# Turning operands by DMA in other portions, and an image's reduction spread over other tiles, in a fused attention and gated feed-forward kernel

## Chip, core and metric

The kernel runs on one core of one Trainium2 chip. The metric is the device time of one execution in microseconds. Before the change three executions took 1033.67, 1035.01 and 1040.39 us; the median is 1035.01 us. The profiled execution took 1032.41 us, of which 1030.6 us lie between its first and its last instruction.

## What is computed

Four images of 384 x 32 pixels with 128 channels serve as keys and values; each is averaged over 4 x 4 pixels and multiplied by a 128 x 128 matrix, which leaves 768 tokens per image. Each image has 12288 queries. Attention is followed by a feed-forward layer with a rectified gate, 1536 wide.

```python
kv_pool = kv.reshape(B, H // r, r, W // r, r, C).mean(axis=(2, 4))
k = v = kv_pool.reshape(B, -1, C) @ w_sr
s = scale * (q @ k.transpose(0, 2, 1))
a = np.exp(s - s.max(-1, keepdims=True))
x = (a / a.sum(-1, keepdims=True)) @ v
gate = np.maximum(x @ w_gate, 0.0)
out = (gate * (x @ w_val)) @ w_out
```

## The kernel before

The 49152 queries are cut into 96 tiles of 512, 24 for each image, and the tiles into groups of four (GRP). A tile passes through a software pipeline. In the main loop (L717), step k works on several tiles at once: scores and exponentials of tile k, weighted values of tile k - 2 (`kV`), the two input projections and the gate of tile k - 3 (`kF`), and the output projection of tile k - 4 (`kO`). The order of all this within a step is a list of words written out by hand; STEADY (L92) serves nearly all steps, FIRST (L82) the first two, DRAIN and LAST the end. The first four tiles and the first image are done before the loop by another list, OPENING. Each word is issued in the order of the list, so that each engine's own queue has the order of the list too.

The words and lines that matter here are these.

- `s0` to `s3`: `score_block` multiplies 128 queries by the 768 keys (L357, two matmuls) into a two-bank PSUM tile. `e0` to `e3`: `exp_block` takes the exponential on ScalarE (L362), whose output `a` has queries on the partitions.
- `a_turn` (L389) turns `a` by a transposing DMA on the SyncE (SP) queue, so that tokens lie on the partitions, as the product with the values needs it. Before the change it follows each `e` word, for one block of 128 queries: 6 blocks of 128 x 128, four times in a step.
- `x0` to `x5`: `values` (L399) multiplies the turned exponentials by the values. In STEADY the first of these, `x1`, stands some four tenths into the step.
- `q_load` (L144) fetches the queries of a group on the GpSimd (POOL) queue, with a cast to 16 bits. `q_turn` (L154) turns a whole group, 16 blocks of 128 x 128, by one DMA on the SP queue, in the second step of the group before.
- `out_turn` and L736 store the output; of the four pieces of a step in the steady part, two go over the SP queue and two over POOL.
- `image_step` (L704) prepares the next image beside the tiles of the present one, in three pairs of 128-token chunks, a pair every four steps. It counts from `at`, which is the step within the image less 6, and for a pair `since = at - 4 * pair`. Loads (L223, two for each of `since` 0 and 1, 512 KB each) go over the SP queue. Sums over pixels (L233 to L241, one half at `since` 2 and one at 3) run on POOL. Word `tb` transposes 32 x 32 blocks on VectorE and stores them to DRAM (L321), and L712 brings them back in four pieces, on the SP queue. Words `P` and `pk` (L298, L307) project and keep the keys. At `since` 8 `turn_values_dma` (L332) turns two chunks of keys into values, by two transposing DMAs on the SP queue.

So the SP queue carries, in one order: the turns of exponentials, of queries and of values, the loads of the image, the trip of the pooled image through DRAM, and half of the output. It takes them strictly one after the other, and each waits there for what it reads. `a` and `aT` have four buffers each, `qT` three, `q16` (the queries before the turn) two, and `kv_in` (the loaded image lines of a pair) two. In the built program each DMA of the SP queue also waits for the landing of the one issued eight before it.

Of the kernel before, what the change touches and what calls it, by code (L numbers as in the profile page):

```python
# [10 lines left out]
FP16 = mybir.dt.float16  # L11
# [5 lines left out]
def kernel(  # L17
# [23 lines left out]
    nc = tc.nc  # L41

    B, N, C = q.shape
# [8 lines left out]
    NS = T // 128  # L52
    NST = N // T
    NT = B * NST
    GRP = 4
# [45 lines left out]
    work = ctx.enter_context(tc.tile_pool(name="work", bufs=2))  # L101
# [19 lines left out]
    q16s, qTs, q32s, q_banks = {}, {}, {}, {}  # L121
# [11 lines left out]
    def q_load(g):  # L133
        if not 0 <= g < NG:
            return
        b, n0 = divmod(g * GRP * T, N)
        q16 = work.tile([128, GRP * NS, C], FP16, tag="q16", bufs=2)
        rows = q[b, n0 : n0 + GRP * T, :]
        if g == NG - 1:
            nc.gpsimd.dma_start(q16, rows.rearrange("(p s) c -> p s c", p=128))  # L140
        else:
            rows = rows.rearrange("(i t j s) c -> j t i s c", i=GRP, t=32, s=NS)
            for j in range(4):
                nc.gpsimd.dma_start(  # L144
                    q16[32 * j : 32 * (j + 1)].rearrange("t (i s) c -> t i s c", i=GRP), rows[j]
                )
        q16s[g] = q16

    def q_turn(g):
        if not 0 <= g < NG:  # L150
            return
        q16 = q16s.pop(g)
        qT = work.tile([128, GRP * NS, 128], FP16, tag="qT", bufs=3)
        nc.sync.dma_start_transpose(qT, q16.rearrange("p s c -> p (s c)"))  # L154
        qTs[g] = qT

    def q_load_pair(i):
        q32 = work.tile([128, 2, NS, C], FP32, tag="kv_s2", bufs=2, name="q32")
# [44 lines left out]
    kv16 = const.tile([128, B, NJC, 2 * C + 16], FP16)  # L203
    kv_in = {}

    def kv_load(b, pair, lines=range(r), queues=(nc.sync,)):
        if (b, pair) not in kv_in:
            if (b, pair) == (0, NJC // 2 - 1):
                kv_in[b, pair] = [
                    work.tile([128, NS * J // 2], FP32, tag="a16", bufs=4, name="kv_line")[  # L210
                        :, 0 : 2 * r * C
                    ].rearrange("p (h dw c) -> p h dw c", h=2, dw=r)
                    for dh in range(r)
                ]
            else:
                lines_in = work.tile([128, r, 2, r, C], FP32, tag="kv_in", bufs=2, name="kv_in")
                kv_in[b, pair] = [lines_in[:, dh] for dh in range(r)]
        parts = kv_in[b, pair]
        rows = kv[b, pair * 2 * HC : (pair + 1) * 2 * HC].rearrange(
            "(hp dh) (wp h dw) c -> dh hp wp (h dw c)", dh=r, h=2, dw=r  # L220
        )
        for dh in lines:
            queues[dh % len(queues)].dma_start(  # L223
                parts[dh].rearrange("p h dw c -> p (h dw c)"), rows[dh]
            )
# [3 lines left out]
    def pool_pixels(eng, b, pair, h):  # L229
        parts = kv_in[b, pair]  # L230
        s2 = work.tile([128, 2, r, C], FP32, tag="kv_s2", bufs=2)
        for i in range(2):
            eng.tensor_tensor(s2[:, i], parts[2 * i][:, h], parts[2 * i + 1][:, h], op=ALU.add)  # L233
        s1 = work.tile([128, r, C], FP32, tag="kv_s1", bufs=2)
        eng.tensor_tensor(s1, s2[:, 0], s2[:, 1], op=ALU.add)
        c2 = work.tile([128, 2, C], FP32, tag="kv_c2", bufs=2)
        eng.tensor_tensor(c2, s1[:, 0:2], s1[:, 2:4], op=ALU.add)
        if h == 0:
            s3s[b, pair] = work.tile([128, 4, 2, 32], FP32, tag="kv_s3", bufs=2, name="kv_s3")
        c4 = c2.rearrange("p i (j c) -> p i j c", c=32)  # L240
        eng.tensor_tensor(s3s[b, pair][:, :, h], c4[:, 0], c4[:, 1], op=ALU.add)  # L241
# [54 lines left out]
    def project(b, pair):  # L296
        pr = project_banks[b, pair] = wide.tile([128, 1024], FP32, tag="wide", name="wide_ps")
        nc.tensor.matmul(  # L298
            pr[:, 0:256].rearrange("c (i h p) -> c i h p", i=4, h=2), w_sr_f32,
            kv_Ts.pop((b, pair)), start=True, stop=True,  # L300
        )
# [25 lines left out]
            for j in range(4)  # L327
        ]

    def turn_values_dma(b, pair):  # L330
        for jc in (2 * pair, 2 * pair + 1):
            nc.sync.dma_start_transpose(kv16[:, b, jc, C : 2 * C], kv16[:, b, jc, 0:C])  # L332


    aTs, x_banks, x16s, xTs, rinvs = {}, {}, {}, {}, {}
    hTs, o_banks, o_sbs, vals = {}, {}, {}, {}
# [50 lines left out]
    def a_turn(k, s0, s1):  # L387
        aT = aTs[k].rearrange("k j t -> k (j t)").rearrange("k (x p) -> k x p", p=128)
        nc.sync.dma_start_transpose(  # L389
            aT[:, s0 * NJC : s1 * NJC], a16s[k][:, s0:s1, :].rearrange("p s j -> p (s j)")  # L390
        )
# [93 lines left out]
    def out_proj(k, fb):  # L485
        if k >= NT - 3:
            if fb == 0:
                o_banks[k] = bank([128, NS, 128])
            for s in range(NS):
                out_add(k, fb, s, o_banks[k][:, s, :], fb == 0 and s == 0)  # L490
            return
        if fb == 0:
            o_banks[k] = bank([128, T])
        nc.tensor.matmul(  # L494
            o_banks[k], wo16[:, fb, :], hTs[k][:, fb, :], start=fb == 0, stop=fb == NFB - 1
        )
# [205 lines left out]
    out_moves, moves, spread = [], [], []  # L702

    def image_step(b, at, step):  # L704
        for pair in range(NJC // 2):
            since = at - 4 * pair
            if since in (0, 1) and step in (2, 8):
                kv_load(b, pair, [2 * since + step // 8])
            elif since in (2, 3) and step == 3:
                pool_pixels(nc.gpsimd, b, pair, since - 2)  # L710
            elif since == 5 and moves and step > 4:
                nc.sync.dma_start(*moves.pop())  # L712
            elif since == 8 and step == 1:
                turn_values_dma(b, pair)

    last = NT + LAG - 1
    for k in range(LEAD, last + 1):  # L717
        g, ph = divmod(k, GRP)
        if k == GRP:
            nc.sync.dma_start_transpose(  # L720
                qTs[1][:, 2 * NS :], q16s.pop(1)[:, 2 * NS :].rearrange("p s c -> p (s c)")
            )
        if ph == 1:
            q_turn(g + 1)
            q_load(g + 2)
        b = k // NST + 1
        at = k % NST - 6
        kO, kF, kV = k - LAG - 1, k - LAG, k - 2
        words = FIRST if kV < LEAD else STEADY if k < NT else DRAIN if k < last else LAST
        for word in words:  # L730
            head, n = word.rstrip("0123456789"), int(word.lstrip("abcdefghijklmnopqrstuvwxyzADPT") or 0)
            if head == "o":
                out_proj(kO, n)
                for queue in (nc.gpsimd, nc.sync):
                    if out_moves and n >= 2:
                        queue.dma_start(*out_moves.pop())  # L736
                if spread:
                    spread_scales(*spread.pop(0))
                if b < B:
                    image_step(b, at, n)  # L740
            elif head == "oT":
                if kO < NT - 3:
                    out_moves = out_turn(kO)
                elif k < last:
                    out_scale(kO, nc.vector, slice(0, NS))
                    out_store(kO, slice(0, NS))
            elif head in ("v", "y", "g", "h"):
                if kF < NT:
                    {"v": value_proj, "y": keep_value, "g": gate_proj, "h": gated}[head](kF, n)
            elif head in ("s", "e"):  # L750
                if k < NT:
                    {"s": score_block, "e": exp_block}[head](k, n)
                    if head == "e":
                        a_turn(k, n, n + 1)
            elif head == "r":
                if LEAD < k <= NT and k % 2 == 0:
                    invert(k - 2)
                    spread += [(k - 2, j) for j in range(4)]
            elif head in ("tb", "P", "pk"):
                pair, since = divmod(at - 5 if head == "tb" else at - 7, 4)  # L760
                if b < B and 0 <= pair < NJC // 2 and since == 0:
                    if head == "tb":
                        moves.extend(turn_blocks(b, pair))
                    elif head == "P":
                        project(b, pair)
                    else:
                        keep_projected(b, pair)
            elif LEAD <= kV < NT:
                if head == "x":
                    values(kV, n)  # L770
                else:
                    keep_values(kV)
# [33 lines left out]
```

The softmax here doesn't subtract the row's maximum and nothing guards it: scores larger than these inputs give would overflow.

## Time and profile before

| engine | busy us | share of the span |
|---|---|---|
| TensorE, matmuls (PE) | 1019.9 | 99% |
| ScalarE (ACT) | 920.8 | 89% |
| VectorE (DVE) | 862.9 | 84% |
| GpSimd (POOL) | 524.5 | 51% |
| TensorE, weight loads (PEld) | 489.2 | 47% |

| issued on the SP queue | count | what one moves | median us from issue to landing |
|---|---|---|---|
| turn of exponentials, L389 | 368 | 6 blocks of 128 x 128 | 3.4 |
| output, L736 | 216 | 64 KB in most | 2.3 |
| load of the image, L223, in the loop and before it | 42 | 512 KB | 4.7 |
| turn of queries, L154 | 22 | 16 blocks | 8.9 |
| turn of values, L332 | 18 | 1 block | 2.6 |

The TensorE clock was granted in full all the time. A busy share is an average over the whole span: it doesn't say whether an engine lost time in a few places, nor how full a queue is. The time in which the SP queue issues a DMA isn't counted as busy time of an engine; it shows only in the timeline, as the duration of the issuing instruction (named SPq).

### The profile page before, as it was taken

The page shows a single profiled execution, that of the slowest core. Times are in us where ns is not written, and L with a number is a line of the kernel's source. Part 1 is how long each engine was busy: PE and PEld are TensorE (multiplying, and loading weights), DVE is VectorE, ACT ScalarE, POOL GpSimd, SP SyncE. Part 2 cuts the span into 40 slices and gives each one's busy share as a digit, 9 for nine tenths or more (in the row PEclk, how much of TensorE's full clock was granted, in tenths as well). Part 3 has the DMA queues.
Part 4 walks back from the last instruction along what each step waited for, and adds up shares of the span by engine and source line. Part 5 has one row for each costly group of instructions (what it writes and reads, how often), then busy time and mean ns, then how long its engine had stood idle before and what let it go on. Part 6 is the DMA issues. An engine that isn't in the chain of part 4 may idle for free.

```text
span 1030.6 us, 18011 instructions
## 1 busy us (share of the span) xinstructions
PE 1019.9 (99%) x5048; PEld 489.2 (47%) x5048; DVE 862.9 (84%) x1432; ACT 920.8 (89%) x1931; POOL 524.5 (51%) x1308
## 2 busy tenths in 40 slices
PE   9999999999999999999999999999999999999998
PEld 6444444444444444444444444444444444444445
DVE  2888888888888888887888888888888888888888
ACT  5999998889999999998999999989899999999986
POOL 3586584834444657564433666566343543343332
PEclk9999999999999999999999999999999999999999
DMA  9998898997989989889888998998997786857541
GB/s 328 130 160 162 173 169 185 143 151 128 160 131 194 155 169 160 159 136 151 145 137 138 185 184 153 180 138 133 147 160 128 137 123 124 145 105 120 103 85 45
DMA packets 480500, 153.55 MB, mean 149 GB/s; under 512 B 456720, under 2 KB 470544, under 8 KB 480400
## 3 DMA queue, kind: packets, MB, share of 16 engines
q1 hardware_dynamic: 458368, 126.10, 67.7%
q0 software_dynamic: 21600, 25.19, 16.0%
q10 hardware_dynamic: 432, 1.11, 0.3%
q8 instruction: 40, 0.66, 0.3%
q14 instruction: 60, 0.49, 0.2%
HBM read 53.94 MB, written 26.35 MB: 78 GB/s over the span
## 4 chain that ended last, share of the span: by engine, by line
PE 96%; DMA 1%; DVE 1%; ACT 1%; issue 0%; SPq 0%; DVEq 0%
PE bank_ps L453 24%; PE bank_ps L466 24%; PE bank_ps L494 23%; PE bank_ps L399 12%; PE wide_ps L357 11%; DVE hT L474 1%; DMA q<-in_q_dram 1%; PE bank_ps L480 1%; DMA aT<-a 1%; PE bank_ps L342 1%; PE bank_ps L416 1%; PE bank_ps L266 0%; PE wide_ps L298 0%; ACT a L362 0%; ACT val L460 0%
## 5 line engine op out<-in xcount | busy, mean ns | idle before, releaser
L474 DVE SCALAR_TENSOR_TENSOR hT<-bank_ps,val 128x512 f16<-128x512 f32 x1152 | 728.9, 680 | 109.3 <-PE bank_ps L466 88.4
L460 ACT CAST val<-bank_ps 128x512 f16<-128x512 f32 x1149 | 628.7, 596 | 44.9 <-PE bank_ps L453 24.6
L453 PE MATMUL bank_ps<-xT,wv 128*128 128x512 f16 x1152 | 420.5, 379 | 0.0
L466 PE MATMUL bank_ps<-xT,wg 128*128 128x512 f16 x1152 | 375.9, 379 | 0.0
L494 PE MATMUL bank_ps<-hT,wo 128*128 128x512 f16 x1116 | 348.4, 379 | 0.0
L362 ACT ACTIVATE a<-wide_ps 128x768 f16<-128x768 f32 x368 | 302.0, 821 | 49.6 <-PE wide_ps L357 49.6
L399 PE MATMUL bank_ps<-aT,kv 128*128 128x512 f16 x552 | 178.9, 379 | 5.5 <-issue 2.0
L357 PE MATMUL wide_ps<-kv,qT 128*128 128x512 f16 x736 | 179.7, 326 | 0.1
L494 PEld LDWEIGHTS <-wo 128*128 128x128 f16 x1116 | 109.2, 98 | 131.7 <-issue 0.3
L466 PEld LDWEIGHTS <-wg 128*128 128x128 f16 x1152 | 112.7, 98 | 121.8
L453 PEld LDWEIGHTS <-wv 128*128 128x128 f16 x1152 | 112.7, 98 | 105.8 <-issue 1.2
L507 POOL TENSOR_TENSOR o_sb<-o_t,scale 128x512 f32<-128x512 f32 x89 | 93.4, 1049 | 132.7 <-issue 119.0
L383 POOL COPY scale<-square 32x8 f32<-32x8 f32 x736 | 141.4, 192 | 28.6
L736 POOL DMA_DIRECT2D out_dram<-o_sb x216 | 134.8, 627 | 18.8 <-POOL o_sb L507 13.0
L357 PEld LDWEIGHTS <-qT 128*128 128x128 f16 x736 | 72.0, 98 | 87.1 <-issue 0.4
L376 POOL TENSOR_TENSOR square<-inverse 128x8 f32<-128x8 f32 x46 | 9.5, 207 | 202.2 <-DVE inverse L374 187.0
L407 DVE CAST xT<-bank_ps 128x512 f16<-128x512 f32 x92 | 63.6, 692 | 33.1 <-PE bank_ps L399 33.1
L399 PEld LDWEIGHTS <-kv 128*128 128x128 f16 x552 | 54.0, 98 | 72.4 <-issue 7.3
L233 POOL TENSOR_TENSOR s<-kv_in 128x512 f32<-128x512 f32 x36 | 45.5, 1273 | 74.0 <-DMA kv_in<-in_kv_dram 73.3
L362 ACT ACTIVATION_READ_ACCUMULATOR a<-wide_ps 128x1 f32 x368 | 75.9, 206 | 0.0
L502 DVE STREAM_TRANSPOSE o_t<-bank_ps 128x512 f32<-128x512 f32 x93 | 65.5, 705 | 0.0
L144 POOL DMA_DIRECT2D q<-in_q_dram x84 | 46.7, 574 | 0.4 <-PE bank_ps L494 0.4
(78 smaller groups left out, 204.9 us busy)
## 6 DMA issues: line engine op xcount, KB each, us to landing
kv_in<-in_kv_dram SPq DMA_DIRECT2D x42, 512.0 KB, 4.7
out_dram<-o_sb SPq DMA_DIRECT2D x177, 64.0 KB, 2.3
out_dram<-o_sb POOLq DMA_DIRECT2D x176, 64.0 KB, 3.3
q<-in_q_dram POOLq DMA_DIRECT2D x84, 128.0 KB, 5.4
aT<-a SPq DMA_TRANSPOSE x368, 3.4
kv_line<-in_kv_dram SPq DMA_DIRECT2D x4, 512.0 KB, 9.8
placed<-blocks SPq DMA_DIRECT2D x9, 128.0 KB, 3.8
kvT<-placed SPq DMA_DIRECT2D x36, 32.0 KB, 1.8
```

The source lines that it names most:

```text
L357: nc.tensor.matmul(s_ps[:, j0 * 128 : j1 * 128], qT, kv16[:, b, j0:j1, 0:C], start=True, stop=True)
L362: nc.scalar.activation(a16s[k][:, s, :], s_banks.pop(s)[:, 0:J], AF.Exp, scale=qk_scale, accum_out=a_sums[k // 2][:, k % 2, s : s + 1],)
L383: nc.gpsimd.tensor_copy(to[32 * b : 32 * (b + 1), :, :, j], squares[k // 2][32 * j : 32 * (j + 1)])
L399: nc.tensor.matmul(x_banks[k], kv16[:, k // NST, jc, C : 2 * C], aT[:, jc], start=first, stop=x_left[k] == 0,)
L453: nc.tensor.matmul(proj_banks["v", k, fb], wv16[:, fb * 128 : (fb + 1) * 128], xTs[k], start=True, stop=True,)
L460: (nc.vector.tensor_copy if k < LEAD - 1 and fb == 5 else nc.scalar.copy)(vals[k, fb], freed(proj_banks.pop(("v", k, fb))))
L466: nc.tensor.matmul(proj_banks["g", k, fb], wg16[:, fb * 128 : (fb + 1) * 128], xTs[k], start=True, stop=True,)
L474: nc.vector.scalar_tensor_tensor(hTs[k][:, fb, :], freed(proj_banks.pop(("g", k, fb))), 0.0, vals.pop((k, fb)), op0=ALU.max, op1=ALU.mult,)
L494: nc.tensor.matmul(o_banks[k], wo16[:, fb, :], hTs[k][:, fb, :], start=fb == 0, stop=fb == NFB - 1)
L502: nc.vector.transpose(o_t, freed(o_banks.pop(k)))
L507: nc.gpsimd.tensor_tensor(to, o_by, scale.to_broadcast([128, NS, 4, 32]), op=ALU.mult)
L736: queue.dma_start(*out_moves.pop())
```

## The change

The change rearranges what goes over the SP queue; the arithmetic stays. Exponentials are turned after every second `e` word, 12 blocks by one DMA. Queries are turned tile by tile, 4 blocks by one DMA in each step, three quarters of a group in the last three steps of the group before and the last quarter in the first step of the group itself. The chain of the next image begins two steps sooner (`at` counts from 4); its sums are taken one step later after the loads than before, so one step sooner on the whole, and so are the trip through DRAM and the projection; the two turns of values of a pair come in two steps, one step sooner and one step later than before. The purpose is a queue with fewer and more even instructions, and data that are there when POOL asks for them.

```diff
-    def q_turn(g):
+    def q_turn(g, i):
         if not 0 <= g < NG:
             return
-        q16 = q16s.pop(g)
-        qT = work.tile([128, GRP * NS, 128], FP16, tag="qT", bufs=3)
-        nc.sync.dma_start_transpose(qT, q16.rearrange("p s c -> p (s c)"))
-        qTs[g] = qT
+        if g not in qTs:
+            qTs[g] = work.tile([128, GRP * NS, 128], FP16, tag="qT", bufs=3, name="qT")
+        at = slice(i * NS, (i + 1) * NS)
+        nc.sync.dma_start_transpose(
+            qTs[g][:, at], q16s[g][:, at].rearrange("p s c -> p (s c)")
+        )
+        if i == GRP - 1:
+            del q16s[g]
...
-    def turn_values_dma(b, pair):
-        for jc in (2 * pair, 2 * pair + 1):
-            nc.sync.dma_start_transpose(kv16[:, b, jc, C : 2 * C], kv16[:, b, jc, 0:C])
-
+    def turn_values_dma(b, jc):
+        nc.sync.dma_start_transpose(kv16[:, b, jc, C : 2 * C], kv16[:, b, jc, 0:C])
...
-            elif since in (2, 3) and step == 3:
-                pool_pixels(nc.gpsimd, b, pair, since - 2)
-            elif since == 5 and moves and step > 4:
+            elif since in (3, 4) and step == 3:
+                pool_pixels(nc.gpsimd, b, pair, since - 3)
+            elif since == 6 and moves and step > 4:
                 nc.sync.dma_start(*moves.pop())
-            elif since == 8 and step == 1:
-                turn_values_dma(b, pair)
+            elif since in (9, 11) and step == 1:
+                turn_values_dma(b, 2 * pair + since // 11)
...
+        if ph == 0 and g > 1:
+            q_turn(g, GRP - 1)
+        elif ph > 0:
+            q_turn(g + 1, ph - 1)
         if ph == 1:
-            q_turn(g + 1)
             q_load(g + 2)
         b = k // NST + 1
-        at = k % NST - 6
+        at = k % NST - 4
...
-                    if head == "e":
-                        a_turn(k, n, n + 1)
+                    if head == "e" and n % 2:
+                        a_turn(k, n - 1, n + 1)
...
-                pair, since = divmod(at - 5 if head == "tb" else at - 7, 4)
+                pair, since = divmod(at - 6 if head == "tb" else at - 8, 4)
```

## Prediction, made before the changed kernel ran

> **What bounds the kernel now.** I read the page's busy times first, then the costliest groups, then the timeline of TensorE step by step, and last the timeline of the SP queue at the places where TensorE stood still. The page first, with the groups of line L357 split by shape:
>
> ```profile
> PE 1019.9 (99%) x5048; PEld 489.2 (47%) x5048; DVE 862.9 (84%) x1432; ACT 920.8 (89%) x1931; POOL 524.5 (51%) x1308
> ```
> ```profile
> L357 PE MATMUL wide_ps<-kv,qT 128*128 128x512 f16 x368 | 139.5, 379 | 0.1
> L357 PE MATMUL wide_ps<-kv,qT 128*128 128x256 f16 x368 | 100.3, 273 | 0.0
> ```
>
> TensorE is busy 99% of the span, so it is the bound, and the question is how much of the rest is to be had. The mean of 379 ns includes the way through the array; what counts is the distance from one start to the next. In the timeline three 512-column matmuls in a row take 0.65 us, so 0.216 us each. A step has 36 + 6 + 4 matmuls of 512 columns and 4 of 256: 46 x 0.2159 + 4 x 0.108 = 10.365 us. I then took the start of the first output matmul (L494) of each step from the timeline. From step 6 to step 94 nearly every step is 10.365 us long, the sum without any gap. Nine steps carry the projection of a pair (L298), 0.43 us more, which stays. Only five are longer beyond that: step 17 by 1.76, step 19 by 1.64, step 21 by 0.58, step 45 by 2.15 and step 69 by 0.16 us. Together 6.29 us: this is all that the steady part loses. The opening and the drain (before 55.7 and after 988 us) aren't touched by the change.
>
> Each of the five gaps stands before the first `values` matmul (L399), which waits for turned exponentials. The largest but one, with weight loads, SP queue and ScalarE around it:
>
> ```profile
> 177.90 0.10 PEld L399 LDWEIGHTS <-kv 128*128 128x128 f16 x1 [2.06 <-issue]
> ```
> ```profile
> 156.39 0.81 ACT L362 ACTIVATE a<-wide_ps 128x768 f16<-128x768 f32 x1 [0.17 <-PE wide_ps L357]
> ```
> ```profile
> 170.80 1.29 SPq L223 DMA_DIRECT2D kv_in<-in_kv_dram  x1
> 172.19 4.06 SPq L389 DMA_TRANSPOSE aT<-a  x3
> 176.35 1.27 SPq L736 DMA_DIRECT2D out_dram<-o_sb  x2
> 177.72 3.94 SPq L389 DMA_TRANSPOSE aT<-a  x3
> 181.83 5.03 SPq L154 DMA_TRANSPOSE qT<-q  x1
> 186.95 1.26 SPq L389 DMA_TRANSPOSE aT<-a  x1
> ```
> ```profile
> 175.94 1.26 POOL L233 TENSOR_TENSOR s<-kv_in 128x512 f32<-128x512 f32 x1 [13.20 <-DMA kv_in<-in_kv_dram]
> ```
>
> The last exponentials of tile 15 were ready at 157.2 us; their turn was issued at 173.47 (the second of the three), 16.3 us later, and landed at 177.84. The matmul went at 177.93. The queue was late, not its data: it went from one DMA to the next with gaps of 0.06 us. Over all tiles this lag, from last exponential to issue, grows while an image is prepared: 4.4 us at tile 5, 10.9 at 9, 16.3 at 15; and it is back at 0.1 us by tile 27, when no image is on the way. The slack before L399 is 16.1 us where nothing lags (tiles 78, 82) and nil in the five gaps. The same lag delays the loads: the load of 170.80 belongs to step 15, and POOL waited 13.2 us for it with the output's scaling behind.
>
> **What the Trainium skill says.** "TensorE: Matmul & The Clock Gate", section "Wait — 56ns, not 53.3ns?", gives 215.7 ns from start to start at 512 columns with a warm array; the trace agrees (0.216), so there is nothing to gain inside a step. "DMA: Bandwidth & Descriptors", section "Rules for kernel authors", tells to coalesce many small transfers into one; the trace agrees for this queue: a turn holds it for a median 1.22 us with 1 block (L332), 1.24 with 6 (L389) and 1.23 with 8 (L720), so these are a price by instruction. The same page, section "Issuing engines are not separate DMA queues", calls a sequencer's time to start a DMA small against the DMA; here it isn't: 1.24 of 3.4 us, and the sum of these fills the queue.
>
> **The change part by part.** I count the queue's time in a group of four steps, 41.46 us, with 0.06 us between instructions. Before, while an image is prepared:
> - 16 turns of exponentials x 1.30 = 20.8 us
> - one turn of queries, 16 blocks, median 4.92 + 0.06 = 5.0
> - 8 output pieces x 0.65 (median 0.594) = 5.2
> - 4 loads x 0.67 = 2.7, 2 turns of values x 1.28 = 2.6
> - the trip through DRAM: 0.57 + 4 x 0.48 and a wait of some 2.7 (the queue held 23.7 us in 9 trips) = 5.2
>
> Sum 41.5 of 41.46: the queue is full, and every wait in it makes it late for good; without an image 31.0, which lets it recover 2.6 us a step. That is the picture of the lag above.
>
> After: the turns of queries are 4 of 4 blocks, 4 x 1.30 = 5.2, no change in the sum but no more five-microsecond piece. Loads, output and values cost the same. The turns of exponentials are 8, of 12 blocks, and the trace has no such size. From below: 1.24 us, as for 8 blocks. From above: 12/16 of the 4.92 us of 16 blocks, 3.7. The 16-block turns range from 1.9 to 6.5 us, so they are held up by what has not drained yet, and 12 blocks should be held up less. I take 2.0; 8 x 2.06 = 16.5 us (10.4 to 30.1). The sum with an image is 37.4 us (31.3 to 51.0) of 41.46, without one 26.9. So 4 us are left in each group instead of none, and the lag stays at a few microseconds.
>
> What the change adds in waits: the first half of a tile's turn now waits for `e1` in place of `e0`, with output pieces and a load queued behind; that is under 3 us once a step, and only the second half sets the start of L399. Its landing takes longer, between 3.4 us (6 blocks) and 8.9 (16 blocks); I take 6. With a slack of 16.1 us less 3.3 that still leaves 12. The last quarter of the queries is turned three steps before its scores. POOL's load of queries needs the buffer that this quarter frees, a step later: it waits only if the queue is a whole step late.
>
> The image chain: sums now run 3 steps after the first load and 1.4 to 1.5 steps (15 us) after the last, against half a step, with 4.7 us to land; so most of POOL's 73.3 us of waiting for `kv_in` go. That is not on the path itself, but what queued behind it is. The last values are turned in step 23 of an image and needed two steps after its end. No cost.
>
> Sum: the 6.29 us go, nothing is added on TensorE. From the profiled execution that gives 1032.41 - 6.29 = 1026.1. The timed median is 2.6 us above the profiled one; such gaps depend on when DMAs land, so I put half of it, 1.3, down to larger gaps that go too, and half to the measurement: 1035.01 - 6.29 - 1.3 = 1027.4 us.
>
> **Rivals.** *The DMA engines are what is full*, not the queue: bytes and blocks are the same, so the turns of 12 blocks hold the queue as long as two of 6 and the lag stays. For it: the 16 DMA engines' mean share is 0.91 and 0.90 in the two groups from 90 to 173 us and 0.98 from 173 to 225. Against it: the six-block turns mostly cost 1.24 us, not a draining time. Time: the gaps stay, 1033 to 1036, say 1035. *Slower*: loads now start in step 4, beside the first output pieces (16 KB each), and share a step with POOL's load of queries (1 MB read per group); if DMA backlog takes the upper 3.7 us per turn, the group's sum of 51 exceeds 41.46 by 9.5 us and the slack of 16.1 is gone within two groups. If each of the nine pairs then costs a gap like the largest seen, 2.15 us: 1035.0 - 6.3 + 19.4 = 1048. Against it: DMA work is unchanged, and the old order survived at this load. *More than forecast*: if timed runs lose far more in gaps than the profiled one, below 1024.7; against it the floor of 1026.1 above.
>
> **Numbers.** Forecast 0.77, DMA engines full 0.11, slower 0.06, more than forecast 0.06. The range goes from 1025.0, just under the floor, to 1033.0, which takes in partial success (a gap or two left, or the timed surplus staying: 1028.7) and leaves the two bad cases outside. Faster by over 1% means below 1024.66, under the floor: 0.07. Within 1%: 0.86. Slower by over 1%, above 1045.4: 0.07.
>
> **What would show it.** Right: every step of 10.365 us, or 10.80 with a projection; lag under 6 us through all images; 12-block issues near 2 us; POOL's wait for `kv_in` near nil; TensorE still at 99%. Wrong: L399 again waiting for `aT` around steps 15 to 21; 12-block issues over 3.5 us; gaps before L357, which would mean queries turned too late.

## Result and profile after

The changed kernel takes 1028.84 us (median of five, 1028.63 to 1029.29). The kernel before takes 1037.4 us (median of five, the three runs named at the top among them, 1033.67 to 1040.39). The ratio is 0.992, with a 95% interval from 0.9891 to 0.9948: faster by 0.8%, with 0.5% to 1.1% as the interval. The forecast was 1027.4 with a range from 1025.0 to 1033.0. The spread says as much as the median: the five runs of before lie 6.7 us apart, those of after 0.7; in a later measurement on another chip, 30 runs of before lie 12.4 us apart and 20 of after 4.0.

First the page after, with the lines of the engines, of the `values` matmul, of the load of queries and of the first sums of an image; the two that changed most are followed by their lines in the page before. The kernel after is a few lines longer: L401 is the old L399, L391 the old L389, L155 the old L154, L227, L335 and L741 the old L223, L332 and L736.

```profile
PE 1020.5 (99%) x5048; PEld 489.5 (48%) x5048; DVE 862.5 (84%) x1432; ACT 920.1 (90%) x1931; POOL 525.1 (51%) x1308
...
L401 PE MATMUL bank_ps<-aT,kv 128*128 128x512 f16 x552 | 178.8, 379 | 0.7 <-DMA aT<-a 0.6
...
L144 POOL DMA_DIRECT2D q<-in_q_dram x84 | 46.7, 573 | 15.6 <-DMA qT<-q 14.7
L237 POOL TENSOR_TENSOR s<-kv_in 128x512 f32<-128x512 f32 x36 | 45.2, 1285 | 1.5 <-DMA kv_in<-in_kv_dram 0.8
```
```profile
L399 PE MATMUL bank_ps<-aT,kv 128*128 128x512 f16 x552 | 178.9, 379 | 5.5 <-issue 2.0
...
L233 POOL TENSOR_TENSOR s<-kv_in 128x512 f32<-128x512 f32 x36 | 45.5, 1273 | 74.0 <-DMA kv_in<-in_kv_dram 73.3
```

The idle time that ends at L401 (L399 before) is 0.7 us in place of 5.5, and POOL waits 1.5 us before its first sums in place of 74. New is 14.7 us in which POOL waits for turned queries before it loads the next ones.

A finer measure of the gaps is the group of weight loads of the same matmul, in the list of groups of the weight-load engine. After the bar stand the idle time ahead of all of them and the part that a wait explains. First before, then after:

```profile
L399 PEld LDWEIGHTS <-kv 128*128 128x128 f16 x552 | 54.0, 98 | 72.4 <-issue 7.3 <-DMA aT<-a 0.5
```
```profile
L401 PEld LDWEIGHTS <-kv 128*128 128x128 f16 x552 | 54.0, 98 | 66.5 <-issue 1.6
```

In kernels without a gap here this number is 65.1 or 65.2 us, which is the ordinary spacing of weight loads. By step, as in the prediction, the gaps of after are 0.17 us in step 15, 0.81 in step 18 and 0.24 in step 41: 1.22 us of the 6.29 of before. The 0.24 us of step 41 stand in all five profiles that have the image chain begun sooner, whether L401 waits or not. The span fell by 3.1 us, from 1030.6 to 1027.5: 5.07 from the gaps, less 0.75 of an opening that took longer (step 4 begins at 36.4 to 37.4 us in all the kernels here, which are the same up to there) and 1.22 after the last matmul, which the last section takes up. The timed runs fell by 8.6 us, since the profiled run of before, 1032.41 us, is faster than all five timed ones; the experiments give a likely reason.

The SP queue after, in the timeline, around the two turns that steps 15 and 18 waited for (issued at 149.83, and the second of the two from 174.32):

```profile
145.28 3.24 SPq L391 DMA_TRANSPOSE aT<-a  x1
148.56 1.16 SPq L227 DMA_DIRECT2D kv_in<-in_kv_dram  x1
149.83 1.36 SPq L391 DMA_TRANSPOSE aT<-a  x1
151.24 3.04 SPq L155 DMA_TRANSPOSE qT<-q  x1
...
174.32 3.88 SPq L391 DMA_TRANSPOSE aT<-a  x2
178.37 4.49 SPq L155 DMA_TRANSPOSE qT<-q  x1
182.96 1.19 SPq L335 DMA_TRANSPOSE kv<-kv  x1
184.24 1.25 SPq L741 DMA_DIRECT2D out_dram<-o_sb  x2
185.59 5.67 SPq L391 DMA_TRANSPOSE aT<-a  x2
```

The turn of 149.83 was issued 12.6 us after its exponentials were ready. The other was issued at 175.90 and took 12.6 us to land. Behind each stands a four-block turn of queries (L155), which the forecast priced at 1.24 us; it holds the queue 3.04 and 4.49 us here, and so makes later turns late. The queue is still late in the first image (by up to 14.0 us at tile 14, where before had 11.8, and 16.3 at tile 15), but by 5.1 and 6.8 at most in the second and third, where before had 13.7 and 13.8.

### The profile page after: what moved, and what is told of

Read it like the earlier page. It is cut to its first block, busy times and chain, and to the rows that moved or that the text cites. A ratio compares the mean times of both kernels' runs of the same rounds, so it can differ in the third digit from the quotient of the medians.

```text
span 1027.5 us, 17571 instructions
## 1 busy us (share of the span) xinstructions
PE 1020.5 (99%) x5048; PEld 489.5 (48%) x5048; DVE 862.5 (84%) x1432; ACT 920.1 (90%) x1931; POOL 525.1 (51%) x1308
## 4 chain that ended last, share of the span: by engine, by line
PE 97%; DMA 2%; ACT 1%; issue 0%; SPq 0%; DVE 0%; DVEq 0%
PE bank_ps L455 24%; PE bank_ps L468 24%; PE bank_ps L496 23%; PE bank_ps L401 12%; PE wide_ps L359 11%; DMA aT<-a 1%; DMA q<-in_q_dram 1%; PE bank_ps L482 1%; PE bank_ps L344 1%; PE bank_ps L418 0%; PE bank_ps L270 0%; PE wide_ps L302 0%; ACT a L364 0%; PE bank_ps L284 0%; ACT val L462 0%
## 5 line engine op out<-in xcount | busy, mean ns | idle before, releaser
L401 PE MATMUL bank_ps<-aT,kv 128*128 128x512 f16 x552 | 178.8, 379 | 0.7 <-DMA aT<-a 0.6
L741 POOL DMA_DIRECT2D out_dram<-o_sb x216 | 134.8, 627 | 19.0 <-POOL o_sb L509 13.0
L401 PEld LDWEIGHTS <-kv 128*128 128x128 f16 x552 | 54.0, 98 | 66.5 <-issue 1.6
L144 POOL DMA_DIRECT2D q<-in_q_dram x84 | 46.7, 573 | 15.6 <-DMA qT<-q 14.7
```

What stands on the lines that cost most here:

```text
L401: nc.tensor.matmul(x_banks[k], kv16[:, k // NST, jc, C : 2 * C], aT[:, jc], start=first, stop=x_left[k] == 0,)
```

## Experiments

The theory to test: the gaps come from lateness of the SP queue, and what makes it late is the time in which it issues, mostly a price by instruction. Rivals: the 16 DMA engines are what is full; or the image's loads come too late for POOL, and the rest follows. A third, the wait for the landing of the DMA issued eight before, can be put aside by the trace of before: in the main loop that landing was always in at least 0.7 us before the issue.

**Each part alone.** Three kernels are the one before with one part of the change. First the exponentials turned two blocks at a time:

```diff
-                    if head == "e":
-                        a_turn(k, n, n + 1)
+                    if head == "e" and n % 2:
+                        a_turn(k, n - 1, n + 1)
```

> The kernel before, with exponentials turned 12 blocks at a time, and nothing else changed. Queue theory (the SP queue's own issuing time is what makes the turns late): the turns of exponentials take 8 x 2.0 in place of 16 x 1.3 us of a group of four steps, so 4.8 us of 41.46 come free, the lag before L399 stays under the slack of 16 us and most of the gain of the whole change comes from this part: 1028 to 1031 us. DMA theory (the 16 DMA engines are what is full): bytes and blocks are the same, 1033 to 1040 us as before. Lead theory (the image's loads come too late for POOL, and what queues behind it is late): as before, since the loads stay where they were, 1033 to 1040 us.

Then the queries turned tile by tile (the call in the loop; `q_turn` itself is as in the change):

```diff
+        if ph == 0 and g > 1:
+            q_turn(g, GRP - 1)
+        elif ph > 0:
+            q_turn(g + 1, ph - 1)
         if ph == 1:
-            q_turn(g + 1)
             q_load(g + 2)
```

> The kernel before, with queries turned tile by tile, and nothing else changed. Queue theory: four turns of 4 blocks at 1.3 to 2.0 us for one of 16 at 4.9, so the queue is as full as before or up to 3 us a group fuller, with smoother landings: 1033 to 1045 us. DMA theory: no change, 1033 to 1040 us. A theory that the five-microsecond piece is what delays the turns behind it: 1028 to 1032 us.

And the image chain begun sooner and spread, with all that belongs to it (only the core is shown):

```diff
-        at = k % NST - 6
+        at = k % NST - 4
...
-            elif since in (2, 3) and step == 3:
+            elif since in (3, 4) and step == 3:
```

> The kernel before, with the image chain begun two steps sooner and spread, and nothing else changed. Lead theory: POOL's wait for the loaded lines (73 us in the profile before) goes, and with it the gaps before L399: 1028 to 1031 us. Queue theory: POOL's wait goes, but the queue still carries 41.5 us of issuing in 41.46 us, so the turns of exponentials are as late as before: gaps of 4 to 12 us stay, 1031 to 1040 us.

Measured, against the kernel before at 1033.63 us on the same chip:

| part alone | us | ratio, 95% interval | gaps in its profile, us |
|---|---|---|---|
| exponentials by two blocks | 1026.28 | 0.9914 [0.9887, 0.9941] | none |
| queries tile by tile | 1037.2 | 1.0036 [1.0023, 1.005] | 11.65 |
| image chain | 1029.68 | 0.995 [0.9931, 0.997] | 2.07 |

The weight loads of the `values` matmul, with exponentials alone, with queries alone and with the image chain alone:

```profile
L399 PEld LDWEIGHTS <-kv 128*128 128x128 f16 x552 | 54.0, 98 | 65.1
```
```profile
L403 PEld LDWEIGHTS <-kv 128*128 128x128 f16 x552 | 54.2, 98 | 76.6 <-DMA aT<-a 6.9 <-issue 6.1
```
```profile
L397 PEld LDWEIGHTS <-kv 128*128 128x128 f16 x552 | 54.0, 98 | 67.5 <-issue 1.6 <-DMA aT<-a 1.1
```

One line of the change, the turns of twelve blocks, takes all the gaps away, and alone it is some 2.5 us faster than the whole change (across chips). POOL still waits 49 us for the image's lines in that kernel, at no cost: as a cause of the gaps by itself the lead of the loads is out. Yet with the loads earlier alone, the gaps shrink by two thirds. The queue is as late as before in the first image (16.4 us at most), and less late in the second and third (11.4 and 12.0, before 13.7 and 13.8): the chain begun sooner helps, by less, and how it does so isn't settled. Turning queries tile by tile alone makes the kernel slower. So the gain of the whole is about that of one part, less what the others cost beside it.

**Each part undone.** The changed kernel with queries by the group again, and the one with the old image chain; the diffs are those above, reversed. The changed kernel ran beside the second.

> The changed kernel with queries turned by the group again, 16 blocks at once. In the profile after, the 4-block turns cost a mean of 1.99 us each, 8.2 us a group with the gaps between, against 5.0 for one of 16. Queue theory: the queue has some 3 us more to spare in a group, so as fast as the changed kernel or a little faster: 1027.5 to 1029. A theory that the large piece delays what is behind it: 1030 to 1034 us.

> The changed kernel with the image chain as it was before. Queue theory: the sum of the queue's instructions is that of the changed kernel, and the image's part of it costs the same wherever it stands, so 1027 to 1030 us. Lead theory: the loads come too late for POOL again, its waits of 73 us return and with them gaps: 1031 to 1036.

> The changed kernel, on a chip with other kernels beside it. Queue theory, after the runs so far: the turns of queries tile by tile cost the queue some 3 us a group, which in the first image is not to spare, so 1 to 3 us above the kernel without this part (1026.7): 1027.5 to 1029.5. A theory that the first measurement merely came from a slower chip: 1026 to 1027.

Measured: 1026.69 us without the queries' part (0.9918 [0.9886, 0.9949] against 1033.63), 1027.51 without the image's part (0.9929 [0.9912, 0.9946] against 1034.5) and 1029.13 for the whole (0.9943 [0.9927, 0.9958] against 1034.5). Beside the twelve-block turns, the queries' part costs 2.2 us (across chips: 1028.84 less 1026.69) and the image's part 1.6 (on one chip: 1029.13 less 1027.51). That the first measurement merely came from a slower chip is out; but the kernel before took 1033.63, 1034.5 and 1036.05 us in the three measurements of this section, so a part of the 2.2 us can be the chips'. In the profile of this second measurement of the whole change a gap of 2.04 us stands in step 14, where the first has none. Lead theory forecast 1031 to 1036 without the image's part; POOL's waits did return, 55 us, but no gap did.

**Queue or DMA engines?** First, one spare DMA a step in the kernel before, on either side.

```diff
+        if k < NT:
+            spare = work.tile([128, 128], FP16, tag="spare", bufs=2, name="spare")
+            nc.sync.dma_start_transpose(spare, wg16[:, 0:128])
```

> The kernel before, with one spare transposing DMA of one block from and to on-chip memory on the SP queue in each step; its result is not used. It moves 32 KB, about 0.2 us of the 16 DMA engines (128 packets of 24 ns over 16 engines), but holds the queue 1.24 us. Queue theory: a group with an image takes 46.7 us of issuing in 41.46 us, so the lag grows by 1.3 us more a step over the 17 or so steps of each of three images, and all of that is past the slack: 20 us an image, 1060 to 1100 us. DMA theory: 0.02 more of the engines' share, at most a few us: 1033 to 1042.

```diff
+        if k < NT:
+            spare = work.tile([128, 768], FP16, tag="spare", bufs=2, name="spare")
+            nc.gpsimd.dma_start(spare, moe_w_gate[:, 0:768])
```

> The kernel before, with one spare load of 384 KB from DRAM on the GpSimd queue in each step; its result is not used. By the share of the query loads in the trace before (1 MB took 3.6 us of the 16 engines) it costs the DMA engines about 1.3 us a step, as much as the other spare DMA costs the SP queue, and POOL about 0.6 us, and the SP queue nothing. Queue theory: landings get a little later, gaps grow by a few us: 1034 to 1045. DMA theory: the engines' share in the image's steps goes from 0.92 to 1.05, so the lag grows past the slack: 1060 to 1100.

Measured: 1081.38 us with the spare turn on SP (1.0467 [1.0414, 1.052]), 1075.67 with the spare load on POOL (1.0414 [1.0351, 1.0477]). What the SP queue shows for the spare turn, and the weight loads of that kernel:

```profile
L728 SPq DMA_TRANSPOSE spare<-wg x92: 1185/1225/2322, 36.3 to 1034.9; - x92
```
```profile
L399 PEld LDWEIGHTS <-kv 128*128 128x128 f16 x552 | 55.1, 100 | 116.6 <-issue 45.7 <-DMA aT<-a 11.2
```

92 instructions of 1.2 us that move 32 KB each cost 47 us: the queue was full, as the count in the prediction said. But the load that leaves the SP queue alone cost 41 us, where queue theory allowed a few. Its trace shows two things at once. The share of the DMA engines in the steps of the second and third image rises from 0.94 to 1.05 or more (packet times summed over 16 engines, by stretches of steps; over 1 means packets that overlap). And on the SP queue stands a wait that the kernel before has not:

```profile
SPq L154 <- DMA q<-in_q_dram: 51.6, 10, 6.7
```

Turns of queries waited 51.6 us in ten places for their load, which stands behind the spare loads on POOL's queue, and with them waited the turns of exponentials behind. This run therefore can't say how much of its 41 us is full engines and how much a queue behind a late load.

Cleaner is to take away. Once the output pieces of the SP queue go to POOL's queue, so that SP gets free and the engines do the same work; once the pieces of POOL's queue are left out (that half of the output is not written), so that the engines get free and SP doesn't.

```diff
-                for queue in (nc.gpsimd, nc.sync):
+                for queue in (nc.gpsimd, nc.gpsimd if 2 * GRP < k < NT else nc.sync):
```

> The kernel before, with the output pieces that the SP queue issues put on the GpSimd queue, from step 9 on; all four of a step then go there. The SP queue is relieved of 2 x 0.65 us a step, the DMA engines of nothing, POOL (busy half its time) issues 1.3 us more a step. Queue theory: 5.2 us of a group of 41.46 come free, about what the turns of 12 blocks bring, and the gaps before L399 go: 1025 to 1029 us. DMA theory: the engines have the same work, gaps as before: 1031 to 1038.

```diff
-                for queue in (nc.gpsimd, nc.sync):
+                for queue in (None if 2 * GRP < k < NT else nc.gpsimd, nc.sync):
                     if out_moves and n >= 2:
-                        queue.dma_start(*out_moves.pop())
+                        move = out_moves.pop()
+                        if queue is not None:
+                            queue.dma_start(*move)
```

> The kernel before, with the output pieces that GpSimd issues left out from step 9 on, so half of the output is not written. The DMA engines are relieved of some 0.85 us a step (two pieces of 512 packets of 13.3 ns over 16 engines), the SP queue of nothing. Queue theory: the queue's own instructions fill it as before, though those held up by undrained work get shorter: most gaps stay, 1029 to 1036 us. DMA theory: the share in an image's steps falls from 0.94 to 0.86 and the gaps go: 1025 to 1028.

Measured against 1036.05 us: 1027.07 with SP relieved (0.9923 [0.9897, 0.9948]) and 1031.36 with the engines relieved (0.9955 [0.9941, 0.9968]). The weight loads, first with SP relieved, then with the engines relieved:

```profile
L399 PEld LDWEIGHTS <-kv 128*128 128x128 f16 x552 | 54.0, 98 | 65.2
```
```profile
L399 PEld LDWEIGHTS <-kv 128*128 128x128 f16 x552 | 54.3, 98 | 70.3 <-DMA aT<-a 4.5 <-issue 1.4
```

With the queue relieved no gap is left, though the engines are as busy as before (0.96 and 0.95 in the second and third image, before 0.94). With the engines relieved (0.87 and 0.86) step 17 is 7.03 us too long, and timed runs lie between 1027.6 and 1034.1. The Trainium skill, "DMA: Bandwidth & Descriptors", section "Issuing engines are not separate DMA queues", says that another issuing engine saves only the sequencer's time to initiate; here giving back that time was enough to close every gap. The queue's own time is enough as a cause. Relief of the engines brought 4.7 of the 9.0 us that relief of the queue brought, so they may well have a part; but this run also takes two issues a step off POOL, and no run separates the two.

The queue's time can be summed in the traces. In steps 10 to 21 the durations of its DMA instructions, with 0.06 us after each, come to 39.6 us for four steps before, 36.2 with the twelve-block turns alone, 36.7 with SP relieved and 40.7 with the engines relieved; the waits for the trip through DRAM come on top. Of these four, the two that fell are the two without a gap.

The 7.03 us of step 17 are not all waiting. The timeline of TensorE in that kernel, and the stretch behind the gap, where the last three numbers are the granted clock, the DMA share and GB/s:

```profile
180.10 0.58 PE L399 MATMUL bank_ps<-aT,kv 128*128 128x512 f16 x1 [4.06 <-DMA aT<-a]
...
181.54 0.63 PE L399 MATMUL bank_ps<-aT,kv 128*128 128x512 f16 x1
181.97 0.63 PE L466 MATMUL bank_ps<-xT,wg 128*128 128x512 f16 x1
182.40 0.63 PE L453 MATMUL bank_ps<-xT,wv 128*128 128x512 f16 x1
```
```profile
180.00:185.40 5.40, 5.30 (x14) 2.10 (x15) 1.58 (x3) 2.07 (x4) 5.20 (x8) 0.50 0.73 139
```

After a wait of 4.06 us the matmuls start 0.43 us apart in place of 0.216, for some 5 us; that is nearly 3 of the 7.03. Around the gaps in the profile of before, at most 2.15 us, the clock stays at 1.00, so a long gap is paid for twice; how long it must be for that, these runs don't fix. It also shows that the profile of before was a mild run: its mean clock is 1.000, while 82 of the 90 timed runs of that kernel in this section have 0.998 or less, as this profile has (0.997). Most of them probably have such a gap.

**How much did twelve blocks free?** The spare turn again, in the kernel with only the exponentials' part.

> Exponentials turned 12 blocks at a time in the kernel before, nothing else changed, with the spare one-block turn on the SP queue in each step (its result is not used). If this part gains by the queue's time that it frees (1.3 x 16 - 1.9 x 8 = 5.6 us a group), then 5.1 us a group put back bring the gaps back to about those of the kernel before, and not to the 48 us more that the same spare turn cost there: 1029 to 1042 us. If it gains by something else (fewer waits, later or larger landings), it should lose about as much as the kernel before did: 1065 to 1080 us.

Measured: 1033.58 us (1026.77 to 1038.21; 0.9967 [0.9949, 0.9986]), 7 us more than without the spare turn (across chips), where the same turn cost the kernel before 47; its profile has gaps of 3.4 us. The freed time and the one put back are alike, and so are the times: this kernel behaves again like the one before, spread included.

**Why the image's part costs something.** The change moved the image's loads from the last two steps of four to the first two, where the queries' load is. Here the queries' load goes to the last step.

```diff
-        if ph == 1:
+        if ph == 3:
             q_load(g + 2)
```

> The changed kernel, with the load of queries (1 MB, POOL queue) in the last step of a group in place of the second. In the changed kernel the image's loads were moved into the first two steps of a group, so they meet the load of queries; in its trace the second turn of a tile that ends such a first step takes 10 to 12.6 us to land while an image is on the way, against 3.7 to 6 in others. Collision theory: moved apart, those landings shorten, the gaps of steps 14 to 18 go, 1026.5 to 1027.5 us. Otherwise, if the four-block turns of queries alone are what costs the changed kernel its 2 to 3 us: 1028.5 to 1029.5.

Measured: 1027.37 us (1027.17 to 1027.48), against 1028.84 and 1029.13 of the changed kernel in two other measurements, on other chips. The second turns of tiles 12 and 16 landed in 5.4 and 4.1 us, in place of 9.6 and 12.6; the gaps come to 0.32 us, and POOL's wait for turned queries, 14.7 us before the move, is gone. The queue's instructions fall from 39.5 to 36.3 us for four steps (steps 10 to 21), though the longest lag stays, 14.6 us. The forecast of the collision theory came, and the trace of the changed kernel says how the loads collide. A twelve-block turn issued with neither load on its way lands in a median 3.9 us, with an image load on its way in 5.4, with a query load in 6.4, with both in 9.6 (15 turns). With the query load moved, and with the old image chain, no turn meets both. But an image load isn't needed: the turn that took 12.6 us was issued at 175.90, when the last image load had landed (154.3), beside the query load that POOL issued at 175.64, late itself because it waited for turned queries:

```profile
175.64 2.23 POOL L144 DMA_DIRECT2D q<-in_q_dram  x4 [7.25 <-DMA qT<-q]
```

Of all these kernels the one with only the exponentials' part has the lowest median, 1026.28 us; the one without the queries' part, on the same chip, is within its spread. In its steady part there is no gap left to remove.

## Why the prediction was right, and where not

**The bound, the floor and the cause.** The count of 10.365 us a step held: from step 6 to step 94 the profile after has no other excess than the projections and 1.22 us of gaps. That the five gaps are lateness of the SP queue, and that the queue was about full (41.5 of 41.46 us by the count), is what the spare turn (47 us) and the relief by 1.3 us a step (no gap) show.

**Twelve blocks.** Taken at 2.0 us between 1.24 and 3.7; measured a mean of 1.94 and a median of 1.47. As a bound for a single turn the 3.7 fails: 9 of 184 are longer, up to 7.1. Landing taken at 6, measured a median of 4.8, but up to 12.6.

**The step that failed: "the turns of queries are 4 of 4 blocks, 4 x 1.30 = 5.2, no change in the sum".** The price was taken from turns of other sizes as if it belonged to the instruction alone. The view of both kinds of turn after, with lowest, median and highest duration in ns:

```profile
L155 SPq DMA_TRANSPOSE qT<-q x88: 1192/1745/5274, 49.3 to 952.0; - x88
```
```profile
L391 SPq DMA_TRANSPOSE aT<-a x184: 1273/1472/7095, 42.6 to 991.9; - x184
```

The mean is 1.99 us, as the sum over 88 is 174.9. Behind turns of six blocks, in the kernel with this part alone, the median is 1.26. So the price depends on what stands before it: here a four-block turn comes right behind a twelve-block one. That it waits until enough of that has drained would be a reason, but isn't shown: twelve-block turns do take longer while 13 to 18 earlier blocks have not landed (median 2.74 us, against 1.44 with none), but six-block turns in the kernel before stay at a median of 1.27 to 1.28 with 13 to 24 blocks ahead. By this count the queue's sum after is 39.9 us of 41.46 rather than 37.4. The direct sums agree: in steps 10 to 21 the whole change has 39.5 us for four steps, where before had 39.6 and the twelve-block turns alone 36.2, so the four-block turns and the longer holds used up what the twelve-block turns freed. That is why the first image still has a lag of 14 us where "under 6 us through all images" was forecast. The second and third, at 5.1 and 6.8, are about right, though there too the instructions take nearly as long as before (37.0 and 37.8 us in steps 30 to 45); the waits for the trip through DRAM fell from 23.7 to 12.6 us in all. The forecast counted on 4 us of room in each group; in the first image next to nothing came free, and that the gaps nearly went all the same was luck.

**The image chain.** That most of POOL's 73.3 us of waiting for `kv_in` go was right: 0.8 us are left. "No cost" was wrong, by 1.6 us on one chip: whether the loads meet the queries' load was asked only in the rival, and the slack of 12 us was trusted to take it. In the first image, where the queue is latest, it wasn't enough. POOL's load of queries was to wait "only if the queue is a whole step late"; it waited three times, 14.7 us in all, and after the longest wait it ran beside the turn behind the largest gap.

**The sum.** 6.29 us were to go, 5.07 did in the profile. From profile to profile the account is 1032.41 - 5.07 + 0.75 (opening) + 1.22 (after the last matmul) = 1029.3, and the profiled run of after took 1029.29. Of the surplus of timed over profiled runs, 2.6 us before, the forecast put half down to the measurement; all of it went (1028.84 is 0.45 below its profiled run), as it would if longer gaps and the slower clock behind them were all of it. The miss of 1.4 us is the gaps left, the longer opening and the longer end (3.2 us), less 1.75 of surplus that went beyond the forecast. So the number came close by errors that partly cancel.

**Rivals.** *DMA engines full*: no, as the whole cause, by the relief of SP alone; as a part, probably (4.7 us, with POOL relieved too). *Slower* did not come; its mechanism, turns slowed where the loads meet the load of queries, did, at some 1.5 us (across chips) and not 19. *More than forecast* did not come.

## What to carry over

A DMA queue that issues in order has a budget of its own, and no page of busy times here shows it: add up, for one period of the loop, the durations of the issuing instructions with the waits between them, and compare with the period. Where it was full here, one line that makes fewer, larger DMAs, or one that moves some to another queue, brought the whole gain, and further smoothing cost some of it again: each part of such a change should be measured alone. A price per issue is a price in its place: a four-block turn took a median 1.26 us behind six-block turns and 1.75 behind twelve-block ones. And one profile can be a mild run: compare its time and its granted clock with those of the timed runs.

## What was not expected

- The time from the end of the last matmul to the end of the span is 4.45 and 4.48 us in two profiles of the changed kernel, 3.94 and 3.98 in the two others that have both twelve-block turns and queries tile by tile, and 3.1 to 3.6 in those of the nine other variants, and 3.2 before. What ties it to that pair of edits wasn't tried.
- The size of a turn hardly matters to the least time of its issue: 1.19 us at the lowest for 4 blocks, 1.21 for 6, 1.27 for 12. Sixteen blocks at once, in contrast, took at least 1.93 us and a median of 4.92 before, and 5.99 behind twelve-block turns (the kernel without the queries' part), and still that kernel is the faster.
- The spread goes with the gaps. Kernels with none in their profile (1026.28, 1027.07 and 1027.51 us, in 4, 4 and 11 runs) repeat within 1.3 us; the kernel before ranges from 1029.2 to 1041.7 in 30 runs on one chip. The twelve-block kernel with the spare turn has both kinds: its 8 runs with a mean clock of 0.999 or more take 1026.8 to 1030.3 us, the other 12 take 1031.4 to 1038.2.
